# Attention block with softmax tiles on four engines: tiles for GpSimd alone, one rescale exp for two blocks, and a re-tuned instruction order

## The chip, the cores and the metric

The kernel runs on one core of one Trainium2 chip. The metric is the device time of that core in microseconds, lower is better. A profiled execution shows a span that is some 1.7 to 2.2 us shorter than the time reported for the same execution. Every difference from the kernel before comes with its 95% interval or its range.

## The reference

One multi-head attention block, bf16 inputs, S = 2048, D = 448, 16 heads of 28.

```python
qkv = (x @ wqkv).reshape(B, S, 3, H, Dh).transpose(2, 0, 3, 1, 4)
q, k, v = qkv[0], qkv[1], qkv[2]
scores = jnp.einsum("bhqd,bhkd->bhqk", q, k) * (Dh ** -0.5)
p = softmax(scores, axis=-1)
o = jnp.einsum("bhqk,bhkd->bhqd", p, v)
return o.transpose(0, 2, 1, 3).reshape(B, S, D) @ wo
```

The scores are 16 x 2048 x 2048 numbers, which are 1024 tiles of 128 x 512. Making exp of them is nearly the whole cost: in the kernel before ScalarE is busy for 397.7 of 410.2 us, 389.7 of them in 425 exps of tile pairs.

## The kernel before: the parts that matter

The program does not write instructions in a fixed order. At build time it simulates its engines with assumed durations and, at each free moment of an engine, takes the first instruction whose conditions hold (a greedy list schedule). Some sixty constants steer the choice. The order so found is then fixed, a list for each engine.

For the softmax, ScalarE takes pairs of tiles (128 x 1024) with its exp. When a PSUM bank of the three `PD` banks is free, the next tile goes the "polynomial way" instead: three VectorE instructions and one GpSimd multiply make the bits of a bf16 exp.

```python
    def start_tile(n, sop, slot, t):
        # ... (cut)
        lo = PX[slot.idx][:].bitcast(U16)...[:, :, 0]
        p1 = add(Op("DVE", P1, lambda: nc.vector.tensor_scalar(          # DU <- PD
            out=DU[b][:], in0=lo, scalar1=SIG / 65536, scalar2=SIG * (SS - 0.5), op0=ALU.mult, op1=ALU.add),
            deps=[sop] + prevl, prio=n - O1))
        p2 = add(Op("DVE", P1, lambda: nc.vector.scalar_tensor_tensor(   # DV <- PD, DU
            ...), deps=[p1], prio=n - O2, lat=0.22))
        gq = add(Op("POOL", PTT, lambda: nc.gpsimd.tensor_tensor(        # DG <- DV, DU
            out=DG[b][:], in0=DV[b][:], in1=DU[b][:], op=ALU.mult), deps=[p2], prio=n, kind="p", lat=PFIN))
        f = add(Op("DVE", P1, lambda: nc.vector.scalar_tensor_tensor(    # PTD <- PD, DG
            ...), deps=[gq], prio=n - OF, acq=acq))                      # then the bank is free
```

The first window blocks are computed with a preliminary maximum, so their sums are rescaled later: one exp for each of two blocks.

```python
    def task_factor(w):                                                  # called for w = 0 and 1
        # ... eight small matmuls into one PSUM bank
        e = add(Op("ACT", 0.49, lambda: nc.scalar.activation(out=RRB[w][:], in_=bank(task)[:], func=ACT.Exp, ...), deps=[m], prio=0))
```

At the end, sums of the last output rows need PD banks too:

```python
    def late_sums():
        def take(tq, n):
            def f(t):
                if pos[0] < NT - NTAIL or n and any(o.kind == "B" and o.acq is not None for o in static["PE"]):
                    return False                 # "n and": only the first may take a bank while a projection still needs one
                # ... take a free PD bank
```

## Time and profile before

| | before |
|---|---|
| time, median of 3 (range) | 411.78 us (411.56 to 411.96) |
| span of the profiled run, mean granted clock | 410.2 us, 0.999 |
| exps of tile pairs (tiles) on ScalarE | 425 (850) |
| tiles by the polynomial way | 174 |
| last exp ends; from there to the end | 402.50 us; 7.68 us |
| VectorE busy; not busy | 395.5 us; 14.7 us |
| GpSimd busy | 225.3 us (55%) |

Read it as a queue: ScalarE starts at 11.4 us, then one exp follows another every 0.917 us with no gap worth naming, then there is a closing part. The lines for this are shown in the prediction. Two stretches are from the table of busy time by stretch of the kernel before. The columns are the stretch, its length, and for PE, weight loads, VectorE, ScalarE and GpSimd the busy us with the number of instructions; then the granted clock, DMA share and GB/s.

```profile
20.00:60.00 40.00, 36.20 (x290) 14.07 (x290) 39.01 (x69) 40.00 (x46) 20.91 (x18) 1.00 0.22 41
60.00:380.00 320.00, 282.75 (x2034) 90.56 (x2046) 315.78 (x545) 320.00 (x350) 188.60 (x163) 1.00 0.13 31
```

### The profile page before, as it was taken

The numbers are of one execution on the slowest core, as the hardware profiler recorded it, in microseconds if no ns is written. First come the engines' busy times: TensorE is split into PE (matmuls) and PEld (weight loads), VectorE is DVE, ScalarE is ACT, GpSimd is POOL, SyncE is SP. The second block draws the span as 40 slices with busy tenths as digits, with TensorE's granted clock in tenths as the row PEclk, the third lists the DMA queues.
The fourth block names the chain that finished last, engine by engine and source line by source line (L and its number), as shares of the span: only waits on it lengthen the run. The fifth ranks groups of instructions, "written<-read, shape, count | busy, mean of one in ns | idle before, by whom it ended". The sixth has DMA issues, their size and how long they took to land.

```text
span 410.2 us, 7553 instructions
## 1 busy us (share of the span) xinstructions
PE 360.2 (88%) x2602; PEld 120.8 (29%) x2613; DVE 395.5 (96%) x701; ACT 397.7 (97%) x437; POOL 225.3 (55%) x217
## 2 busy tenths in 40 slices
PE   8998989898998989899897988989898898989895
PEld 5333232222232232323222222232222222222232
DVE  6999999999999999999999999999999999999995
ACT  4999999999999999999999999999999999999993
POOL 3046557464656657465555646556464655747560
PEclk9999999999999999999999999999999999999999
DMA  9341031012301001111300000000410000001012
GB/s 217 55 75 30 1 61 29 15 53 45 82 2 37 10 28 30 16 41 28 82 18 26 22 10 30 12 26 21 84 42 5 33 12 26 22 27 47 2 72 90
DMA packets 36213, 16.03 MB, mean 39 GB/s; under 512 B 28816, under 2 KB 33296, under 8 KB 36176
## 3 DMA queue, kind: packets, MB, share of 16 engines
q1 hardware_dynamic: 35568, 15.35, 16.1%
q8 instruction: 20, 0.33, 0.3%
q10 hardware_dynamic: 608, 0.22, 0.2%
q14 instruction: 17, 0.14, 0.1%
HBM read 6.91 MB, written 1.96 MB: 22 GB/s over the span
## 4 chain that ended last, share of the span: by engine, by line
ACT 83%; PE 8%; issue 6%; DVE 1%; ACTq 0%
ACT PTA L1122 82%; PE PA L808 3%; PE PO L978 1%; PE PA L355 1%; PE PO L677 0%; ACT RRB L861 0%; PE PO L606 0%; PE PD L476 0%; DVE XT L387 0%; PE PD L606 0%; PE PD L808 0%; PE PO L476 0%; PE PD L758 0%; PE PD L376 0%; DVE OTL L1244 0%
## 5 line engine op out<-in xcount | busy, mean ns | idle before, releaser
L1122 ACT ACTIVATE PTA<-PA 128x1024 bf16<-128x1024 f32 x425 | 390.8, 1247 | 0.1
L926 POOL TENSOR_TENSOR DG<-DV,DU 128x512 f16<-128x512 f16 x174 | 200.4, 1154 | 166.6 <-DVE DV L923 157.3
L808 PE MATMUL PA<-QB,KB 64*128 64x512 bf16 x850 | 167.3, 380 | 42.4 <-ACT PTA L1122 40.2
L808 PEld LDWEIGHTS <-KB 64*128 64x128 bf16 x1024 | 67.0, 93 | 185.7 <-issue 177.3
L920 DVE TENSOR_SCALAR DU<-PD 128x512 f16<-128x512 uint16 x174 | 117.7, 681 | 2.7 <-PE PD L808 2.2
L923 DVE SCALAR_TENSOR_TENSOR DV<-PD,DU 128x512 f16<-128x512 uint16 x174 | 118.3, 683 | 1.3
L939 DVE SCALAR_TENSOR_TENSOR PTD<-PD,DG 128x512 uint16<-128x512 f32 x174 | 118.2, 680 | 0.2 <-POOL DG L926 0.2
L978 PE MATMUL PO<-PTA,VA 128*32 128x512 bf16 x850 | 84.8, 386 | 0.0
L808 PE MATMUL PD<-QB,KB 64*128 64x512 bf16 x174 | 64.7, 376 | 1.2 <-DVE PTD L939 0.8
L978 PE MATMUL PO<-PTD,VA 128*32 128x512 bf16 x174 | 60.0, 386 | 0.0
L978 PEld LDWEIGHTS <-VA 128*32 128x32 bf16 x1024 | 18.8, 94 | 45.8 <-issue 45.3
L901 POOL TENSOR_TENSOR OT<-OSB,RRB 128x512 bf16<-128x512 f32 x15 | 19.1, 1271 | 5.4 <-DVE PTD L939 1.9
L606 PE MATMUL PO<-XT,WQP 112*128 112x512 bf16 x56 | 18.5, 386 | 0.0
L476 PE MATMUL PO<-XT,WKP 112*128 112x512 bf16 x52 | 16.4, 385 | 0.1
L677 PEld LDWEIGHTS <-XT 112*128 112x128 bf16 x256 | 13.4, 98 | 10.4 <-issue 10.3
L677 PE MATMUL PO<-WV,XT 112*128 112x112 bf16 x208 | 16.0, 214 | 0.1
L1083 PE MATMUL PO<-zrow,zeros 128*128 128x512 bf16 x34 | 12.5, 387 | 0.3 <-issue 0.3
L616 DVE TENSOR_SCALAR QB<-PO,offscol 128x512 bf16<-128x512 f32 x14 | 10.4, 744 | 1.0 <-PE PO L606 0.8
L511 DVE TENSOR_SCALAR KB<-PO,onescol 128x512 bf16<-128x512 f32 x12 | 8.9, 743 | 0.0
L886 DVE COPY OSB<-PO 128x512 f32<-128x512 f32 x13 | 8.9, 684 | 0.0
L758 PE MATMUL PO<-WO,OT 128*128 128x448 bf16 x28 | 8.2, 359 | 0.0
L692 DVE CAST VA<-PO 128x448 bf16<-128x448 f32 x13 | 8.0, 617 | 0.0
(97 smaller groups left out, 120.6 us busy)
## 6 DMA issues: line engine op xcount, KB each, us to landing
RRB<-SCR SPq DMA_DIRECT2D x15, 256.0 KB
QB<-QP SPq DMA_DIRECT2D x56, 32.0 KB
KB<-NK SPq DMA_DIRECT2D x12, 128.0 KB
XS<-in_x_dram SPq DMA_DIRECT2D x3, 448.0 KB
out_dram<-XS SPq DMA_DIRECT2D x3, 448.0 KB
QB<-QB SPq DMA_DIRECT2D x28, 32.0 KB
KB<-KB SPq DMA_DIRECT2D x6, 128.0 KB
WV<-in_wqkv_dram SPq DMA_DIRECT2D x1, 392.0 KB
```

What stands on the lines that cost most here:

```text
L476: ops = chain_mm(CC, lambda cc: nc.tensor.matmul(out=ap(), lhsT=WKP[g][:, cc, :], rhs=XT[sc][cc // 2][0:CK, cc % 2, :], start=(cc == 0), s ...
L606: ops = chain_mm(CC, lambda cc: nc.tensor.matmul(out=ap(), lhsT=WQP[g][:, cc, :], rhs=XT[c][cc // 2][0:CK, cc % 2, :], start=(cc == 0), st ...
L677: nc.tensor.matmul(out=ap()[:, jj * GW:(jj + 1) * GW], lhsT=XT[jq][cc // 2][0:CK, cc % 2, jj * P:(jj + 1) * P], rhs=WV[:, cc, g * GW:(g + ...
L808: nc.tensor.matmul(out=ap, lhsT=KB[g % 2][i // 2][a:a + 64, j * P:(j + 1) * P], rhs=QB[w % NQB][i // 2][a:a + 64, :], start=True, stop=Tru ...
L901: o5 = add(Op("POOL", 1.22, lambda: nc.gpsimd.tensor_tensor(out=OT[g][c][:], in0=OSB[b][:], in1=RRB[b][:], op=ALU.mult), deps=o4, prio=-10 ...
L920: p1 = add(Op("DVE", P1, lambda: nc.vector.tensor_scalar(out=DU[b][:], in0=lo, scalar1=SIG / 65536, scalar2=SIG * (SS - 0.5), op0=ALU.mult ...
L923: p2 = add(Op("DVE", P1, lambda: nc.vector.scalar_tensor_tensor(out=DV[b][:], in0=lo, scalar=65536 * (SS - 0.5 + CE / C3), in1=DU[b][:], o ...
L926: gq = add(Op("POOL", PTT, lambda: nc.gpsimd.tensor_tensor(out=DG[b][:], in0=DV[b][:], in1=DU[b][:], op=ALU.mult), deps=[p2], prio=n, kind ...
L939: f = add(Op("DVE", P1, lambda: nc.vector.scalar_tensor_tensor(out=PTD[st["s"].idx][:].bitcast(U16), in0=PX[slot.idx][:], scalar=EBITS + C ...
L978: nc.tensor.matmul(out=PO[HP * st:HP * (st + 1), :], lhsT=VA[g][:, j, st, :], rhs=r["p"][i][1](), start=first, stop=last, tile_position=(0 ...
L1083: nc.tensor.matmul(out=PO[:], lhsT=zeros[:], rhs=zrow[:], start=first, stop=first, skip_group_check=True)
L1122: nc.scalar.activation(out=PTA[pslot.idx][:, 0:len(ns) * QW], in_=PA[s.idx][:, 0:len(ns) * QW], func=ACT.Exp, bias=ACT_BIAS, scale=ACT_SCALE)
```

## The change

Intent: let GpSimd, half idle, make some softmax tiles almost alone. VectorE copies such a tile from PSUM to SBUF, which frees the bank, and GpSimd does all six steps of the polynomial. Because that takes long, these tiles are taken ten rows (40 tiles) ahead of their turn, and the weighted sums may take the rows of a window in any order. Besides, one exp makes the rescale factors of both blocks, which a DMA through DRAM then spreads. Finally, constants were chosen anew, with an order in which the plan's load of matmuls never falls low. It was meant to keep the clock up.

```diff
+    NG = 3            # SBUF buffers for such tiles
+    GMAX = 1          # how many are open at once
+    LA = 10           # rows ahead
+    LAR = 4
...
-    O1 = 30
-    O2 = 10
+    O1 = 10
+    O2 = 20
...                    # some 25 more constants (NTAIL 12 -> 8, UO 20 -> 40, UQ 16 -> 60, FE 40 -> 48, ...)
-    def task_factor(w):
+    def task_factor():
...                    # the matmuls of both blocks into one bank, half the rows each
+        e = add(Op("ACT", 0.49, lambda: nc.scalar.activation(out=RR[:], in_=bank(task)[:], func=ACT.Exp, scale=ACT_SCALE), ...
+        d = add(Op("SP", 0.5, lambda: nc.sync.dma_start(out=SCRF[:]..., in_=RR[0::hh, :]), deps=[e], prio=-10, lat=2.0))
+        return [add(Op("SP", 0.6, lambda w=w: nc.sync.dma_start(out=RRB[w][:], in_=...SCRF broadcast...), deps=[d], ...)) for w in range(NF)]
...
+    def start_g(n, sop, slot, sg):
+        cp = add(Op("DVE", CPY, lambda: nc.vector.tensor_copy(out=X[:], in_=PX[slot.idx][:]), deps=[sop], prio=n - O1))
+        g1 = ... nc.gpsimd.tensor_scalar(out=GU[:], in0=lo, ...)          # one input
+        g2 = ... nc.gpsimd.tensor_scalar(out=GE[:], in0=lo, ...)          # one input
+        g3 = ... nc.gpsimd.tensor_tensor(out=GV[:], in0=GE[:], in1=GU[:], op=ALU.mult)
+        g4 = ... nc.gpsimd.tensor_tensor(out=GU[:], in0=GV[:], in1=GU[:], op=ALU.mult)
+        g5 = ... nc.gpsimd.tensor_tensor(out=X[:], in0=X[:], in1=GU[:], op=ALU.add)
+        f  = ... nc.gpsimd.tensor_scalar(out=PTD[...], in0=X[:], ...)     # one input
+
+    def ahead(t):
+        if g_open[0] >= GMAX or pos[0] < GBEG or not any(s.free_at <= t + 1e-9 for s in sg_slots):
+            return None
+        k0 = pos[0] // HG
+        for k in range(k0 + LA, k0 + LA + LAR):
...
+            for i in GI:
+                if s_ready(k * HG + i, t):      # keys and queries of that row there, by the plan's clock
+                    return k * HG + i
...                    # pv_op takes any ready row; buffers of the end reuse older ones
```

## The prediction

> **What bounds the kernel now.** I read the page's busy table first, then the groups, then the timeline of one stretch, then the chain of waits.
>
> ```profile
> PE 360.2 (88%) x2602; PEld 120.8 (29%) x2613; DVE 395.5 (96%) x701; ACT 397.7 (97%) x437; POOL 225.3 (55%) x217
> ```
>
> Two engines are full, VectorE (DVE) and ScalarE (ACT); GpSimd (POOL) is the only one with much room. The slices say the same at every time: ACT and DVE stand at 9 from the second slice to the last but one, POOL at 4 to 7, the TensorE clock at 9 throughout.
>
> ```profile
> L1122 ACT ACTIVATE PTA<-PA 128x1024 bf16<-128x1024 f32 x425 | 390.8, 1247 | 0.1
> L926 POOL TENSOR_TENSOR DG<-DV,DU 128x512 f16<-128x512 f16 x174 | 200.4, 1154 | 166.6 <-DVE DV L923 157.3
> L920 DVE TENSOR_SCALAR DU<-PD 128x512 f16<-128x512 uint16 x174 | 117.7, 681 | 2.7 <-PE PD L808 2.2
> L923 DVE SCALAR_TENSOR_TENSOR DV<-PD,DU 128x512 f16<-128x512 uint16 x174 | 118.3, 683 | 1.3
> L939 DVE SCALAR_TENSOR_TENSOR PTD<-PD,DG 128x512 uint16<-128x512 f32 x174 | 118.2, 680 | 0.2 <-POOL DG L926 0.2
> ```
>
> The softmax has 1024 tiles of 128x512. ACT takes 850 of them in 425 pairs; 174 go the polynomial way, each with three DVE instructions and one POOL multiply. ACT sat idle 0.1 us before all its exps together, so the span is its queue. The chain that ended last agrees: 82% of it is line 1122. POOL waited 157 us for DVE.
>
> The mean lengths mislead, since records overlap. The real prices are start-to-start times:
>
> ```profile
> 209.40 0.68 DVE L920 TENSOR_SCALAR DU<-PD 128x512 f16<-128x512 uint16 x1
> 210.12 0.69 DVE L923 SCALAR_TENSOR_TENSOR DV<-PD,DU 128x512 f16<-128x512 uint16 x1
> 210.73 0.68 DVE L920 TENSOR_SCALAR DU<-PD 128x512 f16<-128x512 uint16 x1
> 211.32 0.68 DVE L939 SCALAR_TENSOR_TENSOR PTD<-PD,DG 128x512 uint16<-128x512 f32 x1
> 211.92 0.68 DVE L923 SCALAR_TENSOR_TENSOR DV<-PD,DU 128x512 f16<-128x512 uint16 x1
> ```
>
> A DVE instruction occupies 0.60 us, though its record is 0.68; it is 0.72 where the next reads what this one wrote. I take 1.9 us of DVE for a tile (three times 0.60, and 0.1 for part of that gap). In the chain, exps start at 364.54, 366.37 and 367.29, one or two apart: 0.917 us each, 0.458 a tile.
>
> ```profile
> 34.31 0.86 ACT L861 ACTIVATE RRB<-PD 128x512 f32<-128x512 f32 x1
> 34.79 4.05 ACT L1122 ACTIVATE PTA<-PA 128x1024 bf16<-128x1024 f32 x4
> 38.47 0.86 ACT L861 ACTIVATE RRB<-PO 128x512 f32<-128x512 f32 x1
> 38.94 5.89 ACT L1122 ACTIVATE PTA<-PA 128x1024 bf16<-128x1024 f32 x6
> ```
>
> A rescale exp holds ACT 0.48 us (34.31 to 34.79), not its recorded 0.86. The ledger closes: first exp at 11.38; 425 x 0.917 = 389.7; two rescale exps 0.95; stray delays 0.5; last exp ends at 402.5; closing 7.7; together 410.2. The reported time is 411.78, 1.6 more. Everything below is a change to this ledger.
>
> [...]
> - [...] The trace agrees for two inputs: 1154 ns on POOL for f16 and 1265 to 1272 for the f32 multiplies, against 600 of occupancy on DVE. It has no 512-wide one-input POOL instruction, so that price is open.
> - [...] the 174 POOL multiplies all took 1147 to 1166 ns while DVE was full.
> - [...] The granted clock here is 1.00 in every stretch to 380 us and 0.97 in the last, so there is next to nothing to win.
>
> **The change part by part.**
>
> *GpSimd-only tiles.* One DVE copy brings such a tile from PSUM to SBUF, then POOL does three one-input and three two-input instructions. DVE price 0.6 us (the same 128x512 f32 copy, OSB from PO, records 684 ns, so about 0.60 of occupancy). POOL price: 3 x 1.2 (between 1.15 and 1.27) + 3 x about 0.6 (an estimate: [...]like DVE's 0.60) = 5.4 us. Let G be the number of such tiles and d the ordinary polynomial tiles that DVE must give back to stay balanced. ACT shortens by s = 0.458 (G - d). DVE must shorten as much: s = 1.9 d - 0.6 G. So d = 1.058 G / 2.358 = 0.449 G and s = 0.253 G. Each new tile is worth only a quarter of a microsecond: it takes a tile from ACT, but its copy costs DVE nearly a third of one.
>
> *How many.* POOL works usefully from about 22 to 400 us, 378 us, some 371 after the change; 222 of it is taken (200.4 + 19.1 + 2.5). A new tile adds 5.4 and the 0.449 multiplies given back take 0.52 off: 4.88 net. At 100% use that is 30 tiles, at 95% 27, at 92% 24. A second count: multiplies come every 378/174 = 2.2 us, 2.3 after the change, so there is about one gap of 1.15 us a cycle, room for one two-input or nearly two one-input instructions. A tile takes some 4.7 cycles, 11 us; from tile 40 (near 29 us) to the end, less 22 us of normalisations, that gives 30. The code also holds POOL back for half a microsecond ahead of an expected multiply, keeps only one such tile open until its fifth step, and gives its DVE copy a low priority (position far ahead). So fewer than 30: I choose G = 26, d = 12, 418 or 419 pairs. Gain 26 x 0.253 = 6.6 us.
>
> *Ten rows ahead.* Ten rows are 40 tiles; at 1024 tiles in 391 us, or 2.62 per us, that is 15 us, against the 11 to 14 that a tile needs. Weighted sums may now take rows of a window out of order, so a late tile blocks only the last row. I count nothing for this.
>
> *One exp for both blocks.* It removes one 0.48 us ACT instruction on the bounding queue: -0.5. The DMA through DRAM puts the factors where they are used. Before, the POOL rescale ran right after the exp (35.25), but its result was needed by DVE only at 52.25; [...]. The extra POOL cuts are small. Nothing returns to the path.
>
> *Retuned order.* Tile and weighted-sum order, start and tail constants. The head is 11.4 us[...]; four more late tiles may go to DVE. I count -0.2. As the clock is already 1.00, the "load that never falls low" buys nothing[...].
>
> *Added cost.* [...] PE has slack: filler matmuls on zeros (34 + 11) still run, and exps wait 0.1 us in total. Small DVE waits where a long POOL instruction delays a multiply: +0.5.
>
> Sum on 411.78: -6.6 - 0.5 - 0.2 + 0.5 = -6.8, so 405.0 us.
>
> **The rivals.**
> 1. *POOL becomes a bound and DVE waits.* A 1.2 us POOL step started just ahead of a multiply delays that multiply, the DVE add behind it, and a PSUM bank. For it: the mean gap, 1.15 us, is no longer than the step, and there are only three banks and one spare. Against: the scheduler looks for the next multiply, and DVE has other tiles in hand; today it waited 0.2 us for POOL in all. If every tile cost DVE 0.3 us more, s falls: 26 x 0.458 x 0.3/2.358 = 1.5 us less gain, near 406.5. If one-input POOL steps cost 1 us, a tile costs 6.6 and G is near 20: also 406.5.
> 2. *The gain is larger*: POOL fills to 97%, G = 30, and DVE's spare moments (the 0.12 after dependent pairs) take the copies almost free. With a copy at 0.3, s = 0.458 G (1.9 - 0.3)/2.358 = 0.311 G = 9.3 us, so near 402. For it: low-priority copies suit such gaps. Against: POOL at 97% with priority work in between is hard.
> 3. *Weighted sums stall on a late tile*, PO stays held, the exp outputs fill and ACT waits. For it: 11 to 14 us of service against 15 of lead. Against: 24 output buffers are 12 rows of slack. Only with repeated stalls would it be 410 or more.
> 4. *Hidden anyway*: not possible for ACT, whose queue has no idle time; an exp removed is time removed, provided that the matmuls keep up.
>
> **Range and chances.** G from 18 to 31 at 0.253 gives 4.6 to 7.8; with the 0.5 and half a microsecond either way for start and end, and with part of rivals 1 and 2, 402.5 to 408.3. Two per cent is 8.24 us, a time below 403.5: that needs G above 30 at the computed price, or cheaper copies. I give it 0.23. Slower by 2% would need rival 3 at full strength: 0.02.
>
> **What would show it right or wrong.** Right: 416 to 421 exps still 0.917 apart with no idle time before them; 158 to 167 POOL multiplies; 20 to 30 each of six new POOL instructions, two-input near 1.2 us, one-input near 0.6; POOL busy 335 to 360; one RRB exp; DVE still at 95% or more. A one-input step near 1 us, or DVE waiting over 5 us for POOL, shows rival 1. More than 30 new tiles, or fewer than 0.4 multiplies given back per tile, shows rival 2. Idle time of ACT before exps shows rival 3. The prediction is wrong in kind if ACT is no longer the chain, and wrong in size if G or the ratio d/G is off.

What no trace or run of this case shows of the hardware is cut from this text, and the cuts are marked. No term of the sum is among them: it came to -6.6 - 0.5 - 0.2 + 0.5 = -6.8 us and 405.0 us before the cuts, and so it does after them. The 0.6 us of a one-input GpSimd step, three of which are in the 5.4 us of a tile, is set equal to VectorE's 0.60; the trace of the kernel before has no such step, and the changed kernel measured 0.619. The -0.2 and the +0.5 are guesses. That the DMA through DRAM costs nothing stands on the 17 us from 35.25 to 52.25 alone. In the changed kernel its write is issued at 35.94 us, and the first multiply that uses the factors starts at 46.0, 10.1 us later.

## The result, and the profile after

The changed kernel took 410.20 us (median of 4, 410.02 to 410.47), the kernel before beside it 411.80. The ratio is 0.9962, with a 95% interval of 0.9945 to 0.998. Ratios here are the mean time of one kernel's fast runs over that of the other's in the same rounds, so they are not quite the ratio of the medians. It is 1.6 us faster where 6.8 were predicted, and outside the predicted range. All outputs are right.

The busy table and the groups of the changed kernel:

```profile
PE 359.9 (88%) x2599; PEld 120.2 (29%) x2599; DVE 382.0 (94%) x673; ACT 394.3 (97%) x433; POOL 329.2 (81%) x352
...
L1277 ACT ACTIVATE PTA<-PA 128x1024 bf16<-128x1024 f32 x422 | 387.3, 1183 | 0.4 <-PE PA L854 0.2
L1064 POOL TENSOR_TENSOR DG<-DV,DU 128x512 f16<-128x512 f16 x157 | 179.9, 1156 | 49.5 <-DVE DV L1061 40.4
...
L1058 DVE TENSOR_SCALAR DU<-PD 128x512 f16<-128x512 uint16 x157 | 104.3, 680 | 7.2 <-PE PD L854 6.7
...
L1007 POOL TENSOR_TENSOR SG<-SG,GU 128x512 f32<-128x512 f32 x24 | 27.8, 1157 | 1.2 <-DVE QP L691 0.6
...
L997 POOL TENSOR_SCALAR GU<-SG 128x512 f16<-128x512 uint16 x24 | 14.9, 619 | 7.5 <-DVE SG L990 4.7
L990 DVE COPY SG<-PD 128x512 f32<-128x512 f32 x24 | 16.4, 681 | 4.0 <-PE PD L854 3.8
```

There are 24 GpSimd tiles. Their instructions cost what was supposed: 1157 ns for two inputs, 619 ns for one. ScalarE does three exps fewer (422, with one single: 843 tiles, 7 fewer than 850) and still has next to no idle time ahead of them (0.4 us in all, 0.1 before). But VectorE gave back 17 polynomial tiles (174 to 157), and its busy time fell by 13.5 us instead of staying full. It now waits 7.2 us ahead of the first polynomial step for the score matmul, 2.7 before. VectorE waits for banks with work in them.

The same two stretches of the changed kernel:

```profile
20.00:60.00 40.00, 36.37 (x294) 14.11 (x294) 34.76 (x61) 39.92 (x45) 32.14 (x36) 1.00 0.29 63
60.00:380.00 320.00, 283.26 (x2045) 90.33 (x2044) 310.06 (x532) 319.77 (x350) 277.83 (x273) 1.00 0.13 29
```

VectorE is not busy for 5.2 us in the first 40 us (1.0 before) and 9.9 us in the next 320 (4.2 before). The sum over the whole span went from 14.7 to 26.4 us. The balance formula gives d = 0.449 x 24 = 10.8 tiles given back, and 17 were: 6.2 are missing. With an idle time I of VectorE the formula reads d = (1.058 G + I) / 2.358, so the added 11.7 us account for 5.0 of the 6.2.

One place of it is plain. VectorE's instructions of the changed kernel near 32 us (start, length, instruction, and in brackets the idle time before it and what ended it):

```profile
31.83 0.68 DVE L1077 SCALAR_TENSOR_TENSOR PTD<-PD,DG 128x512 uint16<-128x512 f32 x1
35.90 0.69 DVE L990 COPY SG<-PD 128x512 f32<-128x512 f32 x1 [3.39 <-PE PD L854]
...
37.80 0.69 DVE L1058 TENSOR_SCALAR DU<-PD 128x512 f16<-128x512 uint16 x1 [0.68 <-PE PD L854]
```

And the matmuls of the same stretch of the changed kernel:

```profile
31.84 0.39 PE L522 MATMUL PD<-XT,WKP 112*128 112x512 bf16 x1
...
32.48 0.40 PE L909 MATMUL PD<-QB,FW 32*32 32x512 bf16 x4
...
34.26 0.57 PE L723 MATMUL PD<-WV,XT 112*128 112x112 bf16 x8
```

All three PD banks are held by other work: a key projection, the new factor matmuls, a value projection. No softmax tile can reach VectorE for 3.4 us. The rescale exp itself behaved as predicted; ScalarE of the changed kernel:

```profile
34.52 0.77 ACT L916 ACTIVATE RR<-PD 128x512 f32<-128x512 f32 x1
35.00 4.87 ACT L1277 ACTIVATE PTA<-PA 128x1024 bf16<-128x1024 f32 x5
```

It holds the queue for 0.48 us, once instead of twice.

Then the end. The last exp ends at 399.21 us, 3.29 earlier than before, but the span is only 1.78 shorter, since the closing part grew from 7.68 to 9.19 us. VectorE at the end of the kernel before:

```profile
401.66 1.15 DVE L762 TENSOR_TENSOR XS<-PD,KB 128x448 bf16<-128x448 f32 x2
403.08 0.72 DVE L820 STREAM_TRANSPOSE DT<-PO 128x512 f32<-128x512 f32 x1 [0.27 <-PE PO L978]
```

VectorE at the end of the changed kernel:

```profile
400.81 0.62 DVE L808 TENSOR_TENSOR XS<-PD,KB 128x448 bf16<-128x448 f32 x1 [0.79 <-PE PD L804]
401.35 0.71 DVE L866 STREAM_TRANSPOSE SG<-PO 128x512 f32<-128x512 f32 x1
```

And its matmuls there:

```profile
399.84 0.74 PE L888 MATMUL PD<-WO,OT 128*128 128x448 bf16 x3
400.42 0.35 PE L804 MATMUL PD<-WO,OT 128*128 128x448 bf16 x1
```

Before, the transposition that opens the closing part came 0.58 us after the last exp (403.08 - 402.50), released by the last weighted sum. After, it comes 2.14 us after (401.35 - 399.21): it stands in VectorE's queue behind an output addition (L808), which waited 0.79 us for its projection (L804), which the list puts behind the late sums (L888). From the transposition to the end both kernels need the same (7.10 and 7.05 us), so the 1.5 us are all here.

The ledger of the change is then: 7 tiles, that is 3.5 pair exps of 0.917 us each, -3.2; start -0.07; one rescale exp -0.48; left over +0.5; end +1.5; together -1.8 in the span.

### The profile page after: what moved, and what is told of

Read it like the earlier page. It is cut to its first block, busy times and chain, and to the rows that moved or that the text cites. A ratio compares the mean times of both kernels' runs of the same rounds, so it can differ in the third digit from the quotient of the medians.

```text
span 408.4 us, 7572 instructions
## 1 busy us (share of the span) xinstructions
PE 359.9 (88%) x2599; PEld 120.2 (29%) x2599; DVE 382.0 (94%) x673; ACT 394.3 (97%) x433; POOL 329.2 (81%) x352
## 4 chain that ended last, share of the span: by engine, by line
ACT 55%; PE 25%; DVE 11%; issue 7%; DMA 1%; DVEq 0%; ACTq 0%
ACT PTA L1277 54%; PE PA L854 9%; PE PO L1122 7%; PE PD L854 3%; DVE DU L1058 2%; DVE DV L1061 2%; DVE PTD L1077 1%; DMA QB<-QP 1%; PE PO L652 1%; PE PA L393 1%; DVE QB L678 1%; PE PO L1238 1%; DVE QB L662 1%; DVE KB L549 1%; DVE KB L557 1%
## 5 line engine op out<-in xcount | busy, mean ns | idle before, releaser
L1064 POOL TENSOR_TENSOR DG<-DV,DU 128x512 f16<-128x512 f16 x157 | 179.9, 1156 | 49.5 <-DVE DV L1061 40.4
L1058 DVE TENSOR_SCALAR DU<-PD 128x512 f16<-128x512 uint16 x157 | 104.3, 680 | 7.2 <-PE PD L854 6.7
L1061 DVE SCALAR_TENSOR_TENSOR DV<-PD,DU 128x512 f16<-128x512 uint16 x157 | 104.5, 678 | 0.6
L1003 POOL TENSOR_TENSOR GV<-GE,GU 128x512 f16<-128x512 f32 x24 | 27.8, 1159 | 2.5 <-DVE QP L691 0.8
L1005 POOL TENSOR_TENSOR GU<-GV,GU 128x512 f16<-128x512 f16 x24 | 27.8, 1156 | 1.5 <-DVE QP L691 0.8
L1007 POOL TENSOR_TENSOR SG<-SG,GU 128x512 f32<-128x512 f32 x24 | 27.8, 1157 | 1.2 <-DVE QP L691 0.6
L997 POOL TENSOR_SCALAR GU<-SG 128x512 f16<-128x512 uint16 x24 | 14.9, 619 | 7.5 <-DVE SG L990 4.7
L990 DVE COPY SG<-PD 128x512 f32<-128x512 f32 x24 | 16.4, 681 | 4.0 <-PE PD L854 3.8
L652 PE MATMUL PO<-XT,WQP 112*128 112x512 bf16 x56 | 18.7, 386 | 0.4 <-DVE KB L549 0.4
L1020 POOL TENSOR_SCALAR PTD<-SG 128x512 uint16<-128x512 f32 x24 | 14.9, 620 | 3.0 <-DVE QP L691 1.9
L1000 POOL TENSOR_SCALAR GE<-SG 128x512 f32<-128x512 uint16 x24 | 14.9, 619 | 1.9
(105 smaller groups left out, 194.2 us busy)
```

What stands on the lines that cost most here:

```text
L652: ops = chain_mm(CC, lambda cc: nc.tensor.matmul(out=ap(), lhsT=WQP[g][:, cc, :], rhs=XT[c][cc // 2][0:CK, cc % 2, :], start=(cc == 0), st ...
L1003: g3 = add(Op("POOL", PTT, lambda: nc.gpsimd.tensor_tensor(out=GV[:], in0=GE[:], in1=GU[:], op=ALU.mult), deps=[g2], prio=prio + 2, kind=" ...
L1005: g4 = add(Op("POOL", PTT, lambda: nc.gpsimd.tensor_tensor(out=GU[:], in0=GV[:], in1=GU[:], op=ALU.mult), deps=[g3], prio=prio + 3, kind=" ...
L1007: g5 = add(Op("POOL", PST, lambda: nc.gpsimd.tensor_tensor(out=X[:], in0=X[:], in1=GU[:], op=ALU.add), deps=[g4], prio=prio + 4, kind="g", ...
L1058: p1 = add(Op("DVE", P1, lambda: nc.vector.tensor_scalar(out=DU[b][:], in0=lo, scalar1=SIG / 65536, scalar2=SIG * (SS - 0.5), op0=ALU.mult ...
L1064: gq = add(Op("POOL", PTT, lambda: nc.gpsimd.tensor_tensor(out=DG[b][:], in0=DV[b][:], in1=DU[b][:], op=ALU.mult), deps=[p2], prio=n, kind ...
```

## The experiments

My theory after the result, which the runs bear out only in part: the price of a GpSimd tile was right, and the gain was given back by the rest of the new order, which without the tiles is slower than the order before. Rivals: the tiles themselves cost more (GpSimd's steps delay the multiplies and hold banks); the load-conscious order costs something that an order without that care would save.

**1. The one-exp part alone, in the kernel before.**

```diff
# kernel before, with task_factor(), FW, RR, SCRF, negm as in the change; nothing else
-    factor = [task_factor(w) for w in range(NF)]
+    factor = task_factor()
```

> The kernel before with the one-exp part of the change alone (factor matmul, one exp, DMA spread), its constants untouched. My prediction priced this part at -0.48 us, nothing returning: 411.3 us. Rival: any new event makes the order-building code place everything after it differently, and the lot it draws decides more than the 0.48. The program built here holds 426 exps and 172 polynomial tiles in place of 425 and 174, so by the rival +0.92 - 0.48 = +0.4 or more: 412.2 to 413.2 us. The trace should show a single RRB exp of about 0.48 us of occupancy either way.

Measured: 414.08 us, ratio 1.0052 (1.0037 to 1.0067): slower by 2.3 us although an exp is gone. ScalarE has 426 pair exps (425 before), VectorE 172 polynomial tiles (174), and ScalarE was idle 1.3 us ahead of its exps (0.1 before). Of these 1.3 us, 0.87 lie near 85.8 us, 50 us after the task itself. VectorE was not busy for 18.7 us (14.7 before). Removing 0.48 us from a full queue made the kernel slower. That the list schedule re-dealt everything behind it fits these places; it was not separated from a cost of the new task itself. The naive sum of parts fell here.

**2. At most four GpSimd tiles.**

```diff
+    GCAP = 4
-        if g_open[0] >= GMAX or pos[0] < GBEG or ...
+        if g_seq[0] >= GCAP or g_open[0] >= GMAX or pos[0] < GBEG or ...
```

> The changed kernel with everything else the same, but at most 4 GpSimd-only tiles. The program holds 427 exps (854 tiles on ScalarE) and 166 polynomial tiles, against 422 exps and 157 in the changed kernel. If the price I predicted for a GpSimd-only tile is right (0.253 us), taking 20 of 24 away costs 5.1 us: 415 us. If these tiles are worth little in themselves (the rival: GpSimd steps hold up the multiplies, VectorE loses what it gave), it costs 1.6 or less: under 412 us. A time above 411.8 would also say that the rest of the change, without these tiles, is slower than the kernel before.

Measured: 413.83 us, ratio 1.0049 (1.0034 to 1.0064); 166 polynomial tiles, 427 pair exps, last exp ends at 404.02, transposition 0.94 us later. So the other twenty tiles of the changed kernel bring the last exp forward by 4.81 us (404.02 - 399.21), 0.24 each, and give back 9 polynomial tiles, 0.45 each, against the prediction's 0.253 and 0.449. In the time they bring 3.6 us, 0.18 each, because the end grew by 1.2. VectorE was not busy for 24.9 us here too. But its four tiles are copied between 31 and 61 us, and the wait of 3.4 us near 32 us is in this run as well, so only the later twenty tiles are tested, and they add 1.5 us. What they are added to is 2 us slower than the kernel before.

**3. No GpSimd tiles, with the old two order constants.**

```diff
-    GMAX = 1
+    GMAX = 0
-    O1 = 10
-    O2 = 20
+    O1 = 30
+    O2 = 10
```

> The changed kernel without any GpSimd-only tile, and with the two priorities of the polynomial steps as before (30 and 10; with the new ones the order-building code does not come to an end without such tiles). 427 exps, one of them single (853 tiles), 171 polynomial tiles. Prediction's view (the retuned order is worth -0.2 and the one exp -0.5): 411.1 us. Rival (the retuned order loses VectorE tiles and a longer end): 413 to 415 us.

Measured: 414.50 us, ratio 1.0064 (1.0048 to 1.0081); 427 pair exps, 171 polynomial tiles, transposition 2.18 us after the last exp. The long end is there without any GpSimd tile, so the tiles are not needed for it; with the same end constants run 2 had a gap of 0.94. How the end comes out differs from order to order. VectorE was not busy for 21.2 us, between the kernel before (14.7) and the changed kernel (26.4). The factor matmuls stand at the same place (32.53 us), yet VectorE's longest wait there is 1.0 us, not 3.4.

**4. GpSimd tiles with the old two order constants.**

```diff
-    O1 = 10
-    O2 = 20
+    O1 = 30
+    O2 = 10
```

> The same kernel as the run before it (priorities 30 and 10) with the GpSimd-only tiles on: 27 of them, 154 polynomial tiles, 843 tiles on ScalarE. The difference of the two is the value of 27 such tiles in one and the same order. Predicted price: 27 x 0.253 = 6.8 us. By the counts of the two programs ScalarE loses 10 tiles, 4.6 us, and d/G = 17/27 = 0.63. If GpSimd delays cost VectorE time, the difference is under 4 us, with VectorE waiting for GpSimd over 5 us.

Measured: 415.63 us, with a spread from 414.03 to 417.45, ratio 1.0095 (1.0061 to 1.0128). The trace is of the slowest of the four executions. That was a surprise: 27 tiles and the same 422 pair exps as the changed kernel, yet 5 us more. TensorE of this run:

```profile
203.20 0.39 PE L854 MATMUL PD<-QB,KB 64*128 64x512 bf16 x1 [1.57 <-DMA KB<-NK]
```

The busy table by stretch of the same run:

```profile
200.00:204.00 4.00, 2.42 (x12) 0.74 (x11) 3.46 (x6) 3.02 (x4) 2.78 (x3) 1.00 0.81 157
204.00:208.00 4.00, 3.68 (x23) 0.71 (x21) 2.75 (x6) 3.29 (x4) 2.18 (x3) 0.64 0.06 16
208.00:212.00 4.00, 4.00 (x20) 0.59 (x17) 2.96 (x5) 2.71 (x3) 2.66 (x4) 0.50 0.15 37
```

A tile taken ten rows ahead needs the keys of the next head group, whose DMA had not landed. Its matmul stood at the head of TensorE's list for 1.57 us; no other matmul started from 201.24 to 203.20 us, and those of ordinary exps, behind it in the list, stood with it. PE was busy for 2.42 us of those 4. Then the clock was halved for 10.24 us, and exps came 1.45 to 1.6 us apart instead of 0.917. In the fastest execution, 414.03 us, the mean granted clock was 0.995 (0.985 in the traced one), near that of the changed kernel, so the halved clock is not all of the loss.

A part of the delay of these keys is a 128 x 128 VectorE instruction on the way to that DMA. In this run it took 0.98 us there, 0.73 more than the 0.25 of the kernel before, and the wait was 1.57. The group in the kernel before:

```profile
L569 DVE TENSOR_SCALAR NK<-maskm,KMAX 128x128 bf16<-128x128 bf16 x3 | 0.7, 246 | 0.0
```

The group in the changed kernel, where it is lengthened too:

```profile
L615 DVE TENSOR_SCALAR NK<-maskm,KMAX 128x128 bf16<-128x128 bf16 x3 | 2.1, 704 | 0.0
```

All three in the changed kernel start while a GpSimd multiply runs and end 0.04 to 0.06 us after it; one starts at 100.99 us and ends at 101.70, with a multiply from 100.49 to 101.64 beside it. The three of the kernel before had no GpSimd work beside them for more than 0.02 us. What holds the instruction up, no view shows.

**5. The factor task twelve tiles later.** The rival that the load-conscious place of this task costs time.

```diff
-    FE = 48
+    FE = 60
```

> The changed kernel with the factor matmul for the rescale exp placed at tile 60, not 48. In the changed kernel a key task, this factor task and a value task hold all three PSUM banks of the polynomial at 32 to 36 us, and VectorE stands still for 3.4 us. With the shift the program has 159 polynomial tiles and 421 exps (841 tiles) in place of 157 and 422 (843). If the idle stretch is the loss, the time falls by about 0.9 us to 409.3. Against it: the order built has a stretch near 47 to 50 us with only two thirds of the lowest matmul load of the changed kernel. If a low load costs TensorE clock, the granted clock falls under 1.00 in the stretch from 47 to 65 us, exps there come later than 0.917 us, and the time rises to 412 or more.

Measured: 416.17 us, ratio 1.0105 (1.009 to 1.012). The shift did what it was meant to do: VectorE was not busy for 2.8 us from 20 to 60 us (5.2 in the changed kernel), and the two polynomial tiles were gained. The clock did not fall at 47 to 65 us, where the load in the plan was lowest, so that expectation missed. Instead the clock was halved twice for 3.41 us, later. Near 300 us a tile taken ahead had waited 3.14 us for keys (granted clock 0.66 from 300 to 305 us). Near 196 us there was no such wait; the busy table by stretch of this run:

```profile
190.00:195.00 5.00, 3.82 (x19) 0.98 (x19) 5.00 (x10) 5.00 (x7) 4.38 (x6) 1.00 0.02 2
195.00:200.00 5.00, 4.36 (x28) 2.05 (x26) 5.00 (x10) 4.29 (x5) 4.69 (x5) 0.66 0.36 92
```

In the 5 us before the clock fell TensorE was busy for 3.82 us, with no gap above 0.52 us. Low load alone does not explain it: the clock stayed at 1.00 where TensorE was busy for 3.14 us of 5 (47 to 52 us of this run) and for 3.39 of 5 (194.2 to 199.2 us of the kernel before). Why the clock fell near 196 us stays open. So this run doesn't settle its rival, since the falls of the clock hide what the two tiles are worth. And a constant for a task near 35 us had moved work at 200 and 300 us.

**6. The end repaired.**

```diff
-    UO = 40
+    UO = 50
-                if pos[0] < NT - NTAIL or n and any(o.kind == "B" and o.acq is not None for o in static["PE"]):
+                if pos[0] < NT - NTAIL or any(o.kind == "B" and o.acq is not None for o in static["PE"]):
```

> The changed kernel with its end repaired: the late sums of the last window take no PSUM bank while a projection of the window before still needs one, and the last projections may take banks 50 tiles before the end in place of 40. 422 exps (844 tiles), 24 GpSimd-only tiles, 156 polynomial tiles. In the changed kernel the first transposition of the closing part started 2.1 us after the last exp, in the kernel before 0.6. If the wait for the last projection is the cause, the gap is 0.4 to 0.9 us here and the time 409.2 or less. If the end is longer for another reason, it stays at 410.2 to 410.6 (one tile more on ScalarE).

Measured: 409.47 us (409.25 to 410.72), ratio 0.9955 (0.9938 to 0.9971). VectorE at the end:

```profile
400.24 0.72 DVE L866 STREAM_TRANSPOSE SG<-PO 128x512 f32<-128x512 f32 x1 [0.29 <-PE PO L1122]
```

The transposition is released by the weighted sum again, 0.62 us after the last exp, which ends at 399.62. The closing part is repaired; 0.4 us of it is lost again as one tile more went to ScalarE. The long end was a fault of the order, not a cost of the tiles.

**7. Run 4 with the small instruction guarded and later DMA landings assumed.**

```diff
# on top of run 4
-DLAT = 1.4
+DLAT = 1.8
-            out=NK[g][:], ..., prio=prio + 0.2, elig=elig))
+            out=NK[g][:], ..., prio=prio + 0.2, elig=elig, kind="sb"))    # GpSimd keeps off this one
```

> The run with 27 GpSimd-only tiles that took 415.6 us, with two repairs: the VectorE instruction that makes the negated key bounds (NK) is kept apart from GpSimd work, as those that make QP already are, and the order reckons with key transfers that land 0.4 us later. There the NK instructions took 698 to 1084 ns in place of 246, TensorE then waited 1.57 us for the keys of the next group at 201.6 us, and the granted clock was 0.87 in the stretch from 180 to 220 us. 26 GpSimd-only tiles, 153 polynomial tiles, 423 exps. If that chain of causes holds, NK takes about 250 ns again, no matmul waits over 0.5 us for keys, the clock is 1.00 in that stretch and the time 411 to 412 us. If the clock falls for another reason, 414 or more.

Measured: 414.52 us, ratio 1.0073 (1.0058 to 1.0089). The small instruction took 248 ns again and no matmul waited for those keys; which of the two edits did that, the run doesn't say. But the same thing happened with other data. TensorE of this run:

```profile
174.93 0.37 PE L854 MATMUL PD<-QB,KB 64*128 64x512 bf16 x1 [1.71 <-DMA QB<-QP]
```

The clock was halved for 10.24 us after it (mean granted clock of the run 0.986). So the slow instruction was at most one reason for one wait. What the waits have in common is that a tile is taken ahead as soon as the plan believes its data there; run 9 tests that.

**8. A searched order with the end and the guard repaired.** I searched the constants by the plan's own finishing time, and demanded that its load of matmuls stay up.

```diff
+    end as in run 6, guard as in run 7
-    O1 = 10, O2 = 20, UQ = 60, FE = 48, LA = 10, GDEC = 4, ...
+    O1 = 4, O2 = 30, UQ = 40, FE = 54, LA = 11, GDEC = 2, ...
```

> The best order found when the constants of the order-building code are searched anew with the repairs of the two runs before in it, and with no stretch of lower matmul load than the changed kernel has: 421 exps (842 tiles), 26 GpSimd-only tiles, 156 polynomial tiles, the end short. If the changed kernel's small gain is a matter of VectorE tiles lost in the order and of its end, this takes 407.6 to 408.4 us, about 0.9% under the kernel before; over 410 would say that the losses lie elsewhere.

Measured: 412.84 us, ratio 1.003 (1.0015 to 1.0045): a miss. It has 26 tiles and 421 pair exps, but one tile taken ahead waited 2.52 us for keys, and the clock was halved for 6.83 us (0.91 granted from 300 to 340 us). The plan's load was high there; the plan did not know of the wait.

**9. Run 4 with a margin: a tile is taken ahead only if its data have been there for 4 us.**

```diff
# on top of run 4
+    EM = 4.0
-                if s_ready(k * HG + i, t):
+                if s_ready(k * HG + i, t - EM):
```

> The run with 27 GpSimd-only tiles that took 415.6 us (priorities 30 and 10), with one rule more: a tile is taken ahead only if its keys and queries have been ready for 4 us in the order's reckoning. 26 GpSimd-only tiles, 154 polynomial tiles, 844 tiles on ScalarE in 422 exps. Theory: the loss there was a tile taken ahead that stood in TensorE's queue before its keys had landed, TensorE stopped, and the clock was halved. Then no matmul waits 1 us for a DMA here, the clock is 1.00 until the last exp, and the time is 411.0 to 412.0 us; against the run without such tiles in the same order (414.5 us, 853 tiles in 427 exps) that is 3 us for 26 tiles. If waits for DMA are not the cause, the halved clock and 414 us or more remain.

Measured: 409.88 us (409.87 to 409.98), ratio 0.9951 (0.9935 to 0.9968), 5.75 us less than run 4 and under the expected 411 to 412. No score matmul waited for keys or queries. The stretch of run 4's trouble, in this run:

```profile
180.00:220.00 40.00, 36.96 (x279) 12.15 (x272) 38.20 (x67) 40.00 (x45) 33.16 (x33) 1.00 0.17 37
```

The clock is 1.00 and ScalarE is full. Against run 3, which has the same constants and no tiles, 26 tiles bring 4.6 us, 0.18 each.

**10 and 11. All repairs and a searched order.** End, guard and margin (3.0 and 2.5 us), with two sets of constants.

```diff
+    end as in run 6, guard as in run 7, margin as in run 9 (EM = 3.0; run 11: 2.5)
-    UQ = 60, O2 = 20, PARTD = 60, UK = 30, GEND = 0, J0 = 10, J3 = 9, ...
+    UQ = 16, O2 = 30, PARTD = 80, UK = 16, GEND = 4, J0 = 9, J3 = 10, ...
```

> Search of the order's constants with all repairs in: the short end, the guarded NK instruction, tiles taken ahead only when their data have been ready for 3 us, no stretch of lower matmul load than before. 421 exps (842 tiles), 25 GpSimd-only tiles, 157 polynomial tiles. Theory (losses are the end, the late data and the VectorE tiles lost in the order): 407.8 to 408.8 us, under the 409.5 of the run with the end alone repaired. If a halved clock shows again, 411 or more, and the guard against it is not enough.

> A second order of the same search, with data ready for 2.5 us: 421 exps (842 tiles), 26 GpSimd-only tiles, 156 polynomial tiles, a slightly longer end. Same theories: 408.2 to 409.2 us if no data come late, 411 or more if the clock is halved somewhere.

Measured: 407.71 us (407.68 to 407.73), ratio 0.9899 (0.9884 to 0.9913), and 407.53 us (407.44 to 407.67), ratio 0.9895 (0.988 to 0.9909). Run 11 is the best of all and beats both kernels, by 4.3 us and 2.7 us. Run 10 has the factor task at tile 60, as run 5, and run 11 at 48; other constants differ too. The mean granted clock of run 10 was 0.999 in the traced execution, so the late place need not cost the clock.

**12. Run 10 without GpSimd tiles.**

```diff
-    GMAX = 1
+    GMAX = 0
```

> The repaired order that took 407.7 us with its 25 GpSimd-only tiles switched off, all else the same: 427 exps (853 tiles) and 171 polynomial tiles in place of 421 (842) and 157. The difference is the price of 25 such tiles with no halved clock on either side and a short end in both. Predicted price 25 x 0.253 = 6.3 us: 414.0 us. By the counts, 11 tiles of ScalarE fewer: 5.0 us and, with a slightly longer end, 412.2 to 413.2 us. Under 411 us would say that the gain of the repaired order comes from something else than these tiles.

Measured: 413.40 us, ratio 1.0041 (1.0024 to 1.0058). So 25 tiles are worth 5.7 us in run 10, 0.23 each; 6.3 would have been the prediction's price. The busy table without the tiles (run 12):

```profile
PE 358.7 (87%) x2590; PEld 120.4 (29%) x2604; DVE 391.7 (95%) x691; ACT 398.6 (97%) x438; POOL 222.5 (54%) x222
```

And with them (run 10):

```profile
PE 360.0 (89%) x2604; PEld 120.5 (30%) x2604; DVE 381.1 (94%) x674; ACT 393.5 (97%) x432; POOL 334.5 (82%) x358
```

In spans of 411.5 and 405.9 us, VectorE is not busy for 19.8 us without the tiles and 24.8 with them.

All runs together (last exp and gap in us; the gap is from the end of the last exp to the transposition):

| run | time | GpSimd tiles | polynomial tiles | pair exps | last exp | gap |
|---|---|---|---|---|---|---|
| before | 411.78 | 0 | 174 | 425 | 402.50 | 0.58 |
| changed | 410.20 | 24 | 157 | 422 | 399.21 | 2.14 |
| 1 one exp alone | 414.08 | 0 | 172 | 426 | 404.48 | 0.62 |
| 2 four tiles | 413.83 | 4 | 166 | 427 | 404.02 | 0.94 |
| 3 none | 414.50 | 0 | 171 | 427 | 403.57 | 2.18 |
| 4 old order constants | 415.63 | 27 | 154 | 422 | 405.94 | 2.42 |
| 5 factor later | 416.17 | 24 | 159 | 421 | 403.29 | 2.84 |
| 6 end repaired | 409.47 | 24 | 156 | 422 | 399.62 | 0.62 |
| 7 run 4 guarded | 414.52 | 26 | 153 | 423 | 403.65 | 2.18 |
| 8 searched | 412.84 | 26 | 156 | 421 | 403.10 | 0.48 |
| 9 run 4 with margin | 409.88 | 26 | 154 | 422 | 399.38 | 1.77 |
| 10 all repairs | 407.71 | 25 | 157 | 421 | 398.10 | 0.76 |
| 11 all repairs, second order | 407.53 | 26 | 156 | 421 | 398.31 | 0.48 |
| 12 run 10, none | 413.40 | 0 | 171 | 427 | 403.21 | 1.11 |

## Why the prediction was right or wrong

**Right: the bound.** ScalarE's queue stayed full and the exps 0.917 us apart. The ledger still closes, with 0.5 us left over, so the loss could be found in it line by line. The prediction named as a sign against it that ScalarE is no longer the chain. In the chain of the profile's page its share did fall, from 83% to 55%, but with 0.4 us of idle time ahead of all exps its queue is still the bound.

**Half right: the GpSimd tiles, -6.6.** Their number (24, where 26 were chosen) and the length of their instructions were right. The price of one held in one comparison of three:

| pair | tiles | polynomial tiles given back, each | last exp earlier, each | time, each | VectorE not busy |
|---|---|---|---|---|---|
| predicted | 26 | 0.449 | 0.253 | 0.253 | |
| run 2, changed | 20 | 0.45 | 0.24 | 0.18 | 24.9, 26.4 |
| run 3, run 9 | 26 | 0.65 | 0.16 | 0.18 | 21.2, 30.0 |
| run 12, run 10 | 25 | 0.56 | 0.20 | 0.23 | 19.8, 24.8 |

So the agreement of the first pair is in part luck. At 0.18 the 24 tiles are worth 4.3 us, where the prediction had 6.1 with its +0.5 for delays.

**Right: the 0.48 us of one exp as a price on the queue, wrong as a gain.** The removed exp did leave ScalarE 0.48 us. Run 1 shows that the part alone costs 2.3 us; "nothing returns to the path" failed.

**Wrong, and the larger part of the miss: "Retuned order. [...] I count -0.2", with "Nothing returns to the path" (-0.5) and a sum that stands on 411.78.** The sum took the order of the kernel before as a baseline to which terms are added, and counted -0.7 for all that is not tiles. Orders of the new program with no tiles, or four, take 413.4 to 414.5 us (runs 12, 2, 3), 1.6 to 2.7 more than the kernel before. In run 3 this is: 3 tiles more on ScalarE (853 against 850), so that the last exp ends 1.07 us later, and a gap 1.6 us longer. So the sum should have read: 411.8, +2.7 for the rest of the change, -4.3 for the tiles (run 3 to the changed kernel), 410.2. Of the 5.2 us missed, 3.4 are in the rest (+2.7 for -0.7) and 1.8 in the tiles (-4.3 for -6.1).

What these runs don't separate: run 3 has the old O1 and O2, and all three are orders whose constants were chosen with the tiles on, so a part of the +2.7 may be bad luck of the deal without them. All of them also hold the one-exp part, which alone cost 2.3 us in the old order (run 1). No run has the new order without that part, and no order was searched for the new program without tiles. Whether the +2.7 is that part or the other constants is open, and that the kernel before was simply better tuned is argued, not shown. Runs 10 and 11 show what the new program could reach with tiles.

**Rival 1, GpSimd as a new wait, is a part of it.** The prediction's own signs had missed narrowly and all to one side (157 multiplies where 158 to 167 were expected, 422 exps for 416 to 421, GpSimd busy 329 us for 335 to 360, VectorE at 94% instead of 95). The signs named for this rival did not come: VectorE waited 2.2 us for GpSimd multiplies (0.2 before; over 5 was the sign), and a one-input step took 0.62 us. But in all three pairs of the table VectorE's unused time grows with the tiles, by 0.08, 0.34 and 0.20 us a tile, and this rival reckoned with 0.3. The waits that grew most are for score matmuls. That does not acquit GpSimd: by the program a multiply that comes late holds its bank longer, and the next wait could then show as one for a matmul. How much of it is GpSimd and how much the order was not separated.

**Half wrong: the load "buys nothing".** The changed kernel's clock stayed at 1.00 to 380 us; whether its rule of load did that, no run shows. But I took it for a precaution. Runs 4, 5, 7 and 8 show four orders in which tiles taken ahead stopped TensorE and the clock fell, the waits and the clock together costing up to 5.7 us (run 4 against run 9). Waits of 1.57 us (run 4) and 1.71 us (run 7) were each followed by 10.24 us at half clock, one of 2.52 us (run 8) by 6.83 us, and one of 3.14 us (run 5) by 3.41 us. One of 1.10 us (run 4, at 303.8 us) was not: the clock from 300 to 340 us was 1.00. Taking tiles ten rows ahead had a price that my list of rivals lacked: in these four runs a matmul ahead of its data held up what stood behind it in TensorE's list, and the fall of the clock after it added to the price.

**Open.** Why each order loses just the tiles it loses was not settled tile by tile; only the place at 32 us was followed to its banks. Why a removed exp leads to 2 tiles fewer in run 1 is likewise known only as a result. And one fall of the clock, near 196 us in run 5, has no explanation.

## What to carry to other kernels

When a program's order is computed, a change has no sum of parts: test each part with the others switched off inside the new order, not against the old one, and re-tune before judging. Work taken far ahead in an engine's list needs a margin on its data: here waits of 1.57 to 3.14 us stopped what stood behind them and were followed by 3.41 to 10.24 us at half clock, and a margin of 4 us in the plan brought 5.75 us (run 9 against run 4). If an engine that was full has idle time after the change, ask first which buffers or banks kept work from it.
